# Last output tile of a two-stage kernel: one PSUM bank and one copy, or two half banks and two copies

## The chip, the cores and the metric

The kernel runs on one core of one Trainium2 chip. The metric is the device time of one execution in microseconds; of several executions the median is given. The profile comes from one further execution that was recorded instruction by instruction, and its times count from the start of its span.

## What is computed

The first part is attention with a position bias, the second a two-layer network with a squared ReLU. `B, H, S, D` are 4, 8, 576 and 64, so `x` has 2304 rows of 512 and the network's inner width is 2048. Cut to what matters:

```python
def _attn_ref(q, k, v, w1, b1, w2):
    ...
    attn = attn / (np.sum(attn, axis=-1, keepdims=True) + 1e-09)
    return np.matmul(attn, v).astype(np.float32)

def _moe_ref(x, w_in, w_out):
    h = x @ w_in
    r = np.maximum(h, 0.0)
    g = r * r
    return (g @ w_out).astype(np.float32)
```

## The kernel before

The attention takes the first part of the program; the network, which the change touches, takes the rest. Its loop runs over a list `items` of pairs (n, P). Here n says which rows of `x` are worked on: 0 to 3 are the first 512 rows of each batch, and n = B (that is, 4) is the remaining 64 rows of all four batches together, 256 rows in all. P numbers eighths of the inner width. The list is built from `runs` at line 1299, and its last run is (B, 0, 8): the last eight items of the program are the eight values of P for n = B. Nothing is reordered by a planner here: the loop at line 1551 writes its instructions in program order.

For every item, `products` (line 1404) multiplies `x` by its part of the first weight matrix into two PSUM tiles `ha` and `hb`; `sums` and `squares` combine and square them on ACT and DVE; `parts_g` (line 1460) splits the result into a coarse part `gh` (made on ACT, line 1467) and a fine part `gl` (made on DVE, line 1468); and `down` (line 1520) multiplies those by the second weight matrix and adds up in PSUM tiles `y`. A call of `down` belongs to the item before the one whose `products` was written just ahead of it, so TensorE always has the next item's products to do.

For n = B there are two output tiles, k = 0 and k = 1, each of 128 rows by 512 columns, and each fills one PSUM bank. An item adds six matmuls of 512 columns to either of them (two halves f, three products m). In the last item of all, the six for k = 0 are written first and the six for k = 1 after them (the sort at line 1529). When a tile's last matmul has been written, `leave` (line 1492) follows. For n = B it copies the bank to SBUF on DVE with a scale (line 1498) and sends rows 0 to 63 on SP's queue and rows 64 to 127 on ACT's queue (line 1501). Each of these stores moves 64 rows of 512 numbers. The tile `o` in SBUF is one of two buffers that earlier stores used. The program ends when SP has waited for every store (line 1661, where the program is closed).

The PSUM tiles `y0` to `y3` are allocated by name (line 1525). The run before the last one, (3, 6, 8), uses all four; the last run uses `y0` and `y1` only.

Of the kernel before, what the change touches and what calls it, by code (L numbers as in the profile page):

```python
# [10 lines left out]
F32 = mybir.dt.float32  # L11
# [5 lines left out]
AF = mybir.ActivationFunctionType  # L17
ALU = mybir.AluOpType
# [3 lines left out]
B, H, S, D = 4, 8, 576, 64  # L22
# [57 lines left out]
def attention_then_relu2_mlp(ctx: ExitStack, tc: tile.TileContext, q, k, v, cols, w_in, w_out, psi, xmat, dist, out):  # L80
    nc = tc.nc
    PE, DVE, ACT, POOL, SP = nc.tensor, nc.vector, nc.scalar, nc.gpsimd, nc.sync
# [1213 lines left out]
    py_p = ctx.enter_context(tc.tile_pool(name="py", bufs=1, space=PSUM, reuse_waits="tile"))  # L1296
# [6 lines left out]
    firsts = {(n, p0) for n, p0, p1 in runs}  # L1303
    lasts = {(n, p1 - 1) for n, p0, p1 in runs}
# [19 lines left out]
    part_y, ready_y = {}, {}  # L1324
    c_t, g_t, y_t = {}, {}, {}
# [128 lines left out]
    def plain(n, P):  # L1454
        return n < B - 1 and P < NP // 2
# [26 lines left out]
    def pair_tile():  # L1482
        return stage_p["p"].tile([128, 2, 512], F32, name="o", tag="stage", bufs=2)
# [8 lines left out]
    def leave(n, P, k):  # L1492
        y = y_t[n][k]
        j, x = divmod(k, 2)
        unit = 1.0 if plain(n, P) else beta[:, n:n + 1]
        if n == B:
            o = ready_y[j] = pair_tile()
            DVE.tensor_scalar(out=o[:, 0], in0=y, scalar1=unit, scalar2=None, op0=ALU.mult)
            for r, queue in enumerate((SP, ACT)):
                end = S * (2 * k + r + 1)  # L1500
                queue.dma_start(out=out[end - 64:end], in_=o[64 * r:64 * r + 64, 0])
            return
        if (n, 0) in part_y:
            o = ready_y[j]
            DVE.scalar_tensor_tensor(out=o[:, x], in0=y, scalar=unit, in1=o[:, x], op0=ALU.mult, op1=ALU.add)
        else:
            if x == 0:
                ready_y[j] = pair_tile()
            o = ready_y[j]
            ACT.activation(out=o[:, x], in_=y, func=AF.Identity, scale=unit)  # L1510
        if x == 0:
            return
        if P < NP - 1:
            ready_y[j, "dram"] = dram.tile([128, 1024], F32, name=f"py{j}")
            SP.dma_start(out=ready_y[j, "dram"], in_=o.rearrange("p x m -> p (x m)"))
        else:
            rows = out[S * n + 256 * j:S * n + 256 * j + 256].rearrange("(x p) m -> p x m", x=2)
            SP.dma_start(out=rows, in_=o)

    def down(i):  # L1520
        n, P = items[i]
        w = width[n]
        nk = w // 64
        if (n, P) in firsts:
            banks = {k: py_p.tile([128, 512], F32, name=f"y{k}") for k in (2, 3, 0, 1) if k < nk}
            y_t[n] = [banks[k] for k in range(nk)]
        order = [(f, k, m) for f in range(2) for ms in ((0, 1), (2,)) for k in range(nk) for m in ms]
        if i == NI - 1:
            order.sort(key=lambda x: x[1])
        for f, k, m in order:  # L1530
            wh, wl, *fine = w_t[4 * P + 2 + f]
            gh, gl = g_t[i, f]
            t, o = divmod(128 * k, w)
            slot = t if f else 1 - t
            PE.matmul(  # L1535
                y_t[n][k], lhsT=(gl if m == 2 else gh)[:, slot, o:o + 128], rhs=(wh, wl, *fine)[m] if fine else (wh, wl, wh)[m],
                start=((n, P) in firsts and f == 0 and m == 0), stop=((n, P) in lasts and f == 1 and m == 2),
            )
            if (n, P) in lasts and f == 1 and m == 2:
                leave(n, P, k)  # L1540
        if (n, P) in lasts and P < NP - 1:
            for j in range(2):
                part_y[n, j] = ready_y[j, "dram"]

    tmp_p = tmp_stack.enter_context(tc.tile_pool(name="tmp", bufs=1, side="right", reuse_waits="tile"))
    with tc.manual_schedule():
# [4 lines left out]
        for i in range(NI + 1):  # L1551
# [4 lines left out]
            n, P = items[min(i, NI - 1)]  # L1556
# [50 lines left out]
            if i < NI and (n, P) in firsts:  # L1607
                r = run_of[n, P]
# [4 lines left out]
            if i:  # L1613
                down(i - 1)
# [50 lines left out]
```

## Time and profile before

| | |
|---|---|
| median of 3 runs | 681.27 us (680.88 to 681.51) |
| the profiled execution's own time | 681.12 us |
| its span, first to last instruction | 679.3 us |
| PE matmul busy | 662.9 us, 98% |
| PE weight load busy | 509.4 us, 75% |
| DVE busy | 558.6 us, 82% |
| ACT busy | 484.9 us, 71% |
| mean granted TensorE clock | 0.999 |

The span is shorter than the execution's own time because the time also covers what lies before the first and after the last instruction, here 1.8 us. The busy shares are averages over the whole program. The part that the change touches is the last eight items, from about 639 us on, and above all the few microseconds after the last matmul.

### The profile page before, as it was taken

How to read it: one execution, taken by the hardware profiler on the slowest of the kernel's cores; microseconds unless marked ns; L12 is line 12 of the kernel's file. 1: busy time of each engine (PE TensorE's matmuls, PEld its weight loads, DVE VectorE, ACT ScalarE, POOL GpSimd, SP SyncE). 2: the span in 40 equal slices, each digit the busy share in tenths (PEclk: the TensorE clock that was granted, in tenths of full speed). 3: DMA queues.
4: the chain of work that ended last, by engine and by line, in shares of the span. 5: the costliest groups of instructions: out<-in, count | busy, mean ns of one | idle time of the engine just before them, and what ended most of it. 6: DMA issues, size and time to landing. Idle time of an engine off the chain costs nothing.

```text
span 679.3 us, 18939 instructions
## 1 busy us (share of the span) xinstructions
PE 662.9 (98%) x7650; PEld 509.4 (75%) x7650; DVE 558.6 (82%) x1216; ACT 484.9 (71%) x1013; POOL 222.8 (33%) x328
## 2 busy tenths in 40 slices
PE   9999999999999999899999999999999999999997
PEld 8788888887777777678888888887666666666664
DVE  7999899867779978998989879867758886798765
ACT  5779888888787999997566756775676657656321
POOL 2565545442112445455124205144212213331100
PEclk9999999999999999999999999999999999999999
DMA  6674210025073233306741040050038342633101
GB/s 200 196 248 138 94 65 3 2 88 151 11 242 104 52 115 110 104 4 220 292 171 64 32 171 32 5 229 0 1 106 316 110 153 109 226 131 121 66 2 32
DMA packets 34247, 76.67 MB, mean 113 GB/s; under 512 B 7152, under 2 KB 16496, under 8 KB 33136
## 3 DMA queue, kind: packets, MB, share of 16 engines
q1 hardware_dynamic: 34000, 75.21, 32.5%
q8 instruction: 60, 0.98, 0.6%
q14 instruction: 27, 0.22, 0.1%
q10 hardware_dynamic: 160, 0.26, 0.1%
HBM read 57.10 MB, written 18.35 MB: 111 GB/s over the span
## 4 chain that ended last, share of the span: by engine, by line
PE 71%; ACT 10%; DVE 7%; issue 4%; DMA 3%; POOL 3%; SPq 0%; ACTq 0%; POOLq 0%; DVEq 0%
PE y L1535 21%; PE sp L490 10%; PE px L623 10%; PE ha L1416 10%; PE hb L1416 7%; PE bb L430 6%; PE pp L571 4%; ACT pt L1259 3%; DMA r<-in_w_out 3%; ACT p L513 2%; DVE t L506 2%; PE pa L584 1%; POOL wa L804 1%; DVE area L906 1%; ACT o L1510 1%
## 5 line engine op out<-in xcount | busy, mean ns | idle before, releaser
L1416 PEld LDWEIGHTS <-area 128*128 128x128 f16 x1680 | 149.3, 98 | 24.4 <-issue 2.4
L1535 PE MATMUL y<-w,gh 128*128 128x512 f16 (+1 forms) x576 | 142.9, 387 | 0.7 <-ACT gh L1475 0.3
L506 DVE CUSTOM_DVE_ANT_0 t<-sp,area 128x576 f32<-128x576 f32 x144 | 103.7, 752 | 18.7 <-PE sp L490 9.6
L513 ACT ACTIVATE p<-t,negm 128x576 f32<-128x576 f32 x144 | 113.2, 799 | 1.1 <-DVE negm L506 0.9
L490 PE MATMUL sp<-k,q 64*128 64x288 f32 (+1 forms) x608 | 94.7, 427 | 2.6 <-DVE negm L506 1.6
L623 PE MATMUL px<-pt,v 128*64 128x128 f32 (+1 forms) x1600 | 92.2, 266 | 1.2 <-ACT pt L1259 1.2
L623 PEld LDWEIGHTS px<-pt,v 128*64 128x64 f32 x1600 | 79.2, 137 | 12.1 <-ACT pt L1259 8.6
L1416 PE MATMUL ha<-area 128*128 128x256 f16 (+1 forms) x816 | 84.9, 260 | 0.2 <-DVE area L1433 0.2
L445 POOL TENSOR_TENSOR area<-bt,bt 128x256 f32<-128x256 f32 x72 | 65.7, 929 | 55.6 <-DVE bt L438 55.4
L1535 PE MATMUL y<-w,gl 128*128 128x512 f16 (+1 forms) x288 | 77.0, 384 | 0.0
L490 PEld LDWEIGHTS sp<-k,q 64*128 64x128 f32 (+1 forms) x608 | 50.1, 177 | 21.1 <-issue 6.0
L1416 PE MATMUL hb<-area 128*128 128x256 f16 (+1 forms) x612 | 64.7, 260 | 0.0
L833 POOL TENSOR_TENSOR raw<-wa 128x256 f32<-128x256 f32 (+1 forms) x48 | 31.3, 679 | 88.7 <-issue 54.1
L1535 PEld LDWEIGHTS <-gh 128*128 128x128 f16 x344 | 33.1, 98 | 35.6 <-ACT gh L1467 1.1
L417 DVE TENSOR_TENSOR mask<-sdist,theta 128x1024 f16<-128x1024 f16 x81 | 58.0, 718 | 1.1 <-PE bb L430 0.8
L571 PEld LDWEIGHTS pp<-ident,p 64*128 64x128 f32 x1144 | 45.5, 139 | 13.9 <-issue 1.9
L982 ACT COPY pt<-pp 128x512 f32<-128x512 f32 (+1 forms) x76 | 37.4, 544 | 21.5 <-PE pp L571 21.4
L571 PE MATMUL pp<-ident,p 64*128 64x64 f32 x1144 | 50.1, 226 | 2.2 <-DVE raw L832 0.7
L1535 PEld LDWEIGHTS y<-w,gh 128*128 128x128 f32 x232 | 42.5, 188 | 10.2 <-ACT gh L1475 1.0
L430 PEld LDWEIGHTS <-mask 128*128 128x128 f16 x1296 | 46.3, 100 | 4.1 <-issue 1.6
L430 PE MATMUL bb<-wmov,mask 128*128 128x64 f16 x1296 | 47.3, 194 | 0.2 <-ACT pt L982 0.2
L1259 ACT COPY pt<-pp 128x512 f32<-128x512 f32 (+1 forms) x83 | 39.8, 563 | 10.8 <-PE pp L571 10.4
(231 smaller groups left out, 1103.8 us busy)
## 6 DMA issues: line engine op xcount, KB each, us to landing
raw<-in_w_in SPq DMA_DIRECT2D x20, 512.0 KB, 3.9
r<-in_w_out SPq DMA_DIRECT2D x16, 512.0 KB, 7.4
xs<-area SPq DMA_DIRECT2D x4, 1792.0 KB, 9.1
area<-in_w_in SPq DMA_DIRECT2D x12, 512.0 KB, 4.4
py<-o SPq DMA_DIRECT2D x12, 512.0 KB, 4.1
o<-py SPq DMA_DIRECT2D x12, 512.0 KB, 4.3
v<-in_v SPq DMA_DIRECT2D x16, 320.0 KB, 3.3
q<-in_q SPq DMA_DIRECT2D x32, 128.0 KB, 3.5
```

The costliest lines, as they stand in the source:

```text
L417: DVE.tensor_tensor(out=out, in0=win, in1=th, op=ALU.is_ge)
L430: PE.matmul(bb[:, 64 * (7 - r):64 * (8 - r)], lhsT=m[:, r], rhs=wmov[:, n], start=(n == 0), stop=(n == 1))
L445: POOL.tensor_tensor(out=dst, in0=tw, in1=sw, op=ALU.add)
L490: mm = PE.matmul(out_t[to, x, :HALF], lhsT=lhsT, rhs=rhs, start=True, stop=True)
L506: DVE.tensor_tensor_reduce(out=t.rearrange("p (x n) -> p x n", x=2), in0=sp[:, :, :HALF], in1=bias.rearrange("p (x n) -> p x n", x=2), sca ...
L513: ACT.activation(out=p[:, S * n:S * n + S], in_=t, func=AF.Exp, bias=negm[:, n:n + 1], scale=-1.0, accum_out=sums[:, 2 * ic + n:2 * ic + n ...
L571: PE.transpose(dst, p[rows, k0:k0 + 128], ident[rows, rows])
L623: PE.matmul(px[64 * h:64 * h + 64, 128 * m:128 * m + w], lhsT=vt[:, c, h], rhs=src, start=(c == 0), stop=(c == 4))
L982: ACT.copy(dst, src)
L1259: ACT.copy(*c)
L1416: PE.matmul(h[:, s, :w], lhsT=a, rhs=x, start=(k == 0), stop=(k == 5))
L1535: PE.matmul(y_t[n][k], lhsT=(gl if m == 2 else gh)[:, slot, o:o + 128], rhs=(wh, wl, *fine)[m] if fine else (wh, wl, wh)[m], start=((n, P) ...
```

## The change

For n = B the tile k = 1 is kept in two PSUM tiles of 128 rows by 256 columns, which are the first halves of the banks `y1` and `y2`. Every matmul for k = 1 is written as two of 256 columns with the same weights, one for each bank. At the end DVE copies the left half and ACT the right half into the same SBUF tile, and SP's queue sends the left half, ACT's queue the right half; each store now moves 128 rows of 256 numbers. The tile k = 0 is treated as before.

```diff
@@ leave
+        if n == B and k:
+            o = ready_y[j] = pair_tile()
+            rows = out[2 * S * k:2 * S * k + 2 * S].rearrange("(r s) m -> r s m", r=2)[:, S - 64:]
+            DVE.tensor_scalar(out=o[:, 0, :256], in0=y[0], scalar1=unit, scalar2=None, op0=ALU.mult)
+            ACT.activation(out=o[:, 0, 256:], in_=y[1], func=AF.Identity, scale=unit)
+            for x, queue in enumerate((SP, ACT)):
+                queue.dma_start(out=rows[:, :, 256 * x:256 * x + 256], in_=o[:, 0, 256 * x:256 * x + 256])
+            return
         if n == B:
@@ down
-            banks = {k: py_p.tile([128, 512], F32, name=f"y{k}") for k in (2, 3, 0, 1) if k < nk}
+            banks = {k: py_p.tile([128, 512], F32, name=f"y{k}") for k in (2, 3, 0, 1) if k < nk + (n == B)}
             y_t[n] = [banks[k] for k in range(nk)]
+            if n == B:
+                y_t[n][1] = [banks[k][:, :256] for k in (1, 2)]
...
-            PE.matmul(
-                y_t[n][k], lhsT=(gl if m == 2 else gh)[:, slot, o:o + 128], rhs=(wh, wl, *fine)[m] if fine else (wh, wl, wh)[m],
-                start=((n, P) in firsts and f == 0 and m == 0), stop=((n, P) in lasts and f == 1 and m == 2),
-            )
+            lhsT, rhs = (gl if m == 2 else gh)[:, slot, o:o + 128], (wh, wl, *fine)[m] if fine else (wh, wl, wh)[m]
+            start, stop = (n, P) in firsts and f == 0 and m == 0, (n, P) in lasts and f == 1 and m == 2
+            if n == B and k:
+                for x, y in enumerate(y_t[n][k]):
+                    PE.matmul(y, lhsT=lhsT, rhs=rhs[:, 256 * x:256 * x + 256], start=start, stop=stop)
+            else:
+                PE.matmul(y_t[n][k], lhsT=lhsT, rhs=rhs, start=start, stop=stop)
```

On TensorE, in the last item and near the end of the program, the rows before are these (each matmul stands behind the load of its weights; `y1` is the bank of k = 1, and `w31` a tile of the second weight matrix):

```order
L1535 LDWEIGHTS gh_10728
L1535 MATMUL y1_10290<-w31_9472,gh_10728 128x512
L1535 LDWEIGHTS gh_10728
L1535 MATMUL y1_10290<-w31_9472,gh_10728 128x512
L1535 LDWEIGHTS gl_10727
L1535 MATMUL y1_10290<-w31_9472,gl_10727 128x512
```

With the change the same place reads:

```order
L1549 LDWEIGHTS gh_10771
L1549 MATMUL y1_10291<-w31_9472,gh_10771 128x256
L1549 LDWEIGHTS gh_10771
L1549 MATMUL y2_10289<-w31_9472,gh_10771 128x256
L1549 LDWEIGHTS gh_10771
L1549 MATMUL y1_10291<-w31_9472,gh_10771 128x256
L1549 LDWEIGHTS gh_10771
L1549 MATMUL y2_10289<-w31_9472,gh_10771 128x256
L1549 LDWEIGHTS gl_10770
L1549 MATMUL y1_10291<-w31_9472,gl_10770 128x256
L1549 LDWEIGHTS gl_10770
L1549 MATMUL y2_10289<-w31_9472,gl_10770 128x256
```

Each matmul of 512 columns has become two of 256, and each of the two has a weight load of its own: 48 matmuls and 48 weight loads more over the eight items.

On ACT, the end of the program before is this (`o_10737` is the SBUF tile of k = 0, `o_10747` that of k = 1):

```order
L1430 ACTIVATE area_87<-ha_10653,xT0_83 128x4x128
L1467 ACTIVATE gh_10724<-area_87 128x2x128
L1467 ACTIVATE gh_10728<-area_87 128x2x128
L1501 DMA out_0<-o_10737 64x512
L1501 DMA out_0<-o_10747 64x512
```

With the change (`o_10780` is the tile of k = 0, `o_10796` that of k = 1):

```order
L1430 ACTIVATE area_87<-ha_10690,xT0_83 128x4x128
L1467 ACTIVATE gh_10767<-area_87 128x2x128
L1467 ACTIVATE gh_10771<-area_87 128x2x128
L1509 DMA out_0<-o_10780 64x512
L1500 ACTIVATE o_10796<-y2_10289,xT0_83 128x256
L1502 DMA out_0<-o_10796 2x64x256
```

ACT's copy stands behind ACT's store of k = 0 and ahead of its store of k = 1. It waits for the last matmul, and also, in three semaphore instructions of its own, for older DMAs on the tile's buffer. SP's two stores keep their places; DVE's second copy keeps its place and is half as wide.

## Rows read from the trace of the kernel before

**Rows 1.** The page: busy time, share and count of each engine.
```profile
PE 662.9 (98%) x7650; PEld 509.4 (75%) x7650; DVE 558.6 (82%) x1216; ACT 484.9 (71%) x1013; POOL 222.8 (33%) x328
```

**Rows 2.** The chain that ended last, from 640 us: start, length, what.
```profile
659.40 2.59 PE y L1535 x12
661.99 1.34 PE ha L1416 x24
663.33 1.00 PE hb L1416 x18
664.33 2.59 PE y L1535 x12
...
672.12 2.80 PE y L1535 x12
674.92 0.03 issue
674.95 0.75 DVE o L1498
```

**Rows 3.** The timeline after 674.4 us, stores one by one: start, length, what.
```profile
674.43 0.52 SPq L1501 DMA_DIRECT2D out<-o  x1
674.44 0.57 ACTq L1501 DMA_DIRECT2D out<-o  x1
674.53 0.38 PE L1535 MATMUL y<-w,gl 128*128 128x512 f16 x1
675.73 0.49 SPq L1501 DMA_DIRECT2D out<-o  x1
675.73 0.51 ACTq L1501 DMA_DIRECT2D out<-o  x1
```

**Rows 4.** DMA issues, from 675.2 us: how many, size, issue to landing.
```profile
out<-o SPq DMA_DIRECT2D x1, 128.0 KB, 2.4
out<-o ACTq DMA_DIRECT2D x1, 128.0 KB, 2.6
```

**Rows 5.** The timeline of PE, 619 to 640 us: start, length, what.
```profile
619.86 2.78 PE L1416 MATMUL ha<-xT,area 128*128 128x256 f16 x24
622.48 2.13 PE L1416 MATMUL hb<-xT,area 128*128 128x256 f16 x18
...
631.97 1.89 PE L1535 MATMUL y<-w,gh 128*128 128x512 f16 x8
633.70 1.03 PE L1535 MATMUL y<-w,gl 128*128 128x512 f16 x4
...
637.15 1.50 PE L1416 MATMUL ha<-area 128*128 128x128 f16 x24
638.49 1.17 PE L1416 MATMUL hb<-area 128*128 128x128 f16 x18
```

**Rows 6.** Groups by shape, 639 to 680 us: weight loads, their mean ns.
```profile
L1416 PEld LDWEIGHTS <-area 128*128 128x128 f16 x261 | 15.1, 98 | 1.4
L1535 PEld LDWEIGHTS <-gh 128*128 128x128 f16 x64 | 5.9, 98 | 6.3 <-ACT gh L1467 0.8
```

**Rows 7.** The timeline, 636 to 640 us: who leaves and who refills the banks.
```profile
636.70 2.73 DVE L1505 SCALAR_TENSOR_TENSOR o<-y,xT,o 128x512 f32<-128x512 f32 x4 [1.19 <-PE y L1535]
...
639.49 1.03 PE L1535 MATMUL y<-w,gh 128*128 128x512 f16 x4
```

**Rows 8.** Instructions of single lines: ns least/median/most, first and last start.
```profile
L1498 DVE TENSOR_SCALAR o<-y,xT x2: 751/752/752, 673.7 to 674.9; 128x512 f32<-128x512 f32 x2
L1432 DVE SCALAR_TENSOR_TENSOR area<-ha,xT,area x14: 477/743/752, 448.7 to 669.0; 128x512 f32<-128x512 f32 x10, 128x256 f32<-128x256 f32 x4
L1510 ACT ACTIVATE o<-y,xT x4: 670/682/697, 504.1 to 505.8; 128x512 f32<-128x512 f32 x4
L1430 ACT ACTIVATE area<-ha,xT x14: 687/1094/1135, 446.2 to 668.3; 128x1024 f32<-128x1024 f32 x10, 128x512 f32<-128x512 f32 x4
```

**Rows 9.** Semaphore instructions on ACT's queue, lines 1501 and 1467.
```profile
L1501 ACTq EVENT_SEMAPHORE  x2: 17/17/17, 671.8 to 675.0; - x2
L1467 ACTq EVENT_SEMAPHORE  x27: 17/17/38, 475.4 to 671.7; - x27
```

**Rows 10.** DMA issues of the page and of the first 2 us.
```profile
area<-in_psi SPq DMA_DIRECT2D x1, 256.0 KB, 3.1
area<-in_cols SPq DMA_DIRECT2D x1, 37.0 KB, 1.8
```

**Rows 11.** Busy time in stretches; last two numbers: DMA share, GB/s.
```profile
675.70:676.05 0.35, 0.00 (x0) 0.00 (x0) 0.00 (x0) 0.00 (x0) 0.00 (x0) 1.00 1.04 205
677.10:677.45 0.35, 0.00 (x0) 0.00 (x0) 0.00 (x0) 0.00 (x0) 0.00 (x0) 1.00 0.97 181
```

## The prediction

> **What bounds the kernel now.** I read the busy shares first, then the chain that ended last, then the timeline of the end. TensorE's matmuls are busy for 98% of the span [rows 1], so where TensorE runs, only TensorE's work counts. The chain shows this for the place of the change: an item of the last run is 2.59 us of `y` matmuls, 1.34 us of `ha` and 1.00 us of `hb`, back to back, with no wait between them [rows 2]. Copies on DVE and ACT lie beside it and cost nothing there. That ends with the last matmul at 674.92 us. From there on nothing runs beside the chain. DVE takes 0.75 us for its copy of the bank [rows 2], the two stores are issued at 675.73 [rows 3], the slower of them lands 2.6 us later [rows 4], at 678.33, and the remaining 0.97 us to the end of the span at 679.3 is SP's last waits and the closing of the program. So the end after the last matmul is 4.4 us, and a change there moves the time one for one; but 4.4 us of 681 is all there is. A measurement of this kernel can tell about 0.2% from no change, which is 1.36 us.
>
> **TensorE's part.** Over the eight items, 48 matmuls of 512 columns become 96 of 256. The price of a pair against the one it replaces comes from the distances between starts. 24 matmuls of 256 columns, each with its own weight load, take from 619.86 to 622.48, or 109.2 ns each; 8 of 512 columns take from 631.97 to 633.70, or 216.3 ns each [rows 5]. A pair costs 218.3 ns, 2.1 ns more; times 48 that is **0.10 us** longer, on the chain. The extra weight loads are inside the 109.2 ns already, since every matmul of that row has one. That they hide is seen even more sharply with 128 columns: 24 of those start within 1.34 us, 56 ns apart [rows 5], while one weight load there is recorded with 98 ns [rows 6], so successive loads overlap the matmuls and each other.
>
> [...]
>
> The new bank `y2` has to be free before the first item of the run writes to it. DVE empties the four banks of the run before from 636.70 to 639.43, in the order 0, 1, 2, 3, so `y2` is the third, free at about 638.7 [rows 7]; the first matmul of the run starts at 639.49, and the tile k = 1 comes two matmuls later. This wait costs nothing, with 0.7 us to spare. If the cover went, at most the fourth copy would have to end, still before 639.49.
>
> **The two copies.** DVE: a copy of 512 columns takes 0.75 us, and DVE's other reads of PSUM take 0.74 us for 512 columns and 0.48 for 256 [rows 8]. So the left half takes 0.48 us. It may start one half matmul earlier than now, since the left half's last matmul is the one before the last: 0.11 us ahead of 674.92, so 674.81, plus the 0.03 us from matmul to DVE. DVE ends at 675.32 and SP's store goes out at **675.35**, 0.38 us earlier than now.
>
> ACT: 512 columns of `y` with a scale take 0.68 us [rows 8]. 1024 columns take 1.09 us and 512 take 0.69 on line 1430 [rows 8], so 256 columns fewer save 0.2 us, and the right half takes 0.47 us. What is ahead of it on ACT decides when it starts: ACT's own store of k = 0 is issued from 674.44 for 0.57 us, to 675.01 [rows 3], and the next instruction on ACT's queue is recorded at 675.0 [rows 9]. ACT is therefore not free when the last matmul ends at 674.92. Then come the three semaphore instructions for older DMAs; their DMAs ended long ago, but they take 17 to 38 ns each plus a step between them [rows 9]. I put 0.1 us for all three. The copy starts at 675.12, ends at 675.59, and ACT's store goes out at **675.62**, only 0.11 us earlier than now. The bounds are 675.45 (if ACT were free at 674.95) and 675.73 (if each of the three took 0.07), so from 0.28 us earlier to no gain.
>
> **The two stores.** They carry as many bytes as now, as 128 rows of 1 KB instead of 64 rows of 2 KB each, and no row of the trace shows that form going to memory. From below the bound is the load of 128 short rows, 37 KB, at the quiet start, 1.8 us from issue to landing; from above, 256 KB in 128 rows, 3.1 us [rows 10]. Now the two stores are issued at the same moment and land after 2.4 and 2.6 us [rows 4], and while their data move the DMA engines are full (a share of 1.04 and 0.97 in the busiest stretches) [rows 11]. With the change ACT's store comes 0.27 us behind SP's and finds the engines partly drained. I take 2.2 us for it, a little under SP's 2.4 and above the quiet 1.8. ACT's store then lands at 677.82, SP's at 675.35 plus 2.4, so 677.75. The later one counts, 677.82 against 678.33 now: **0.51 us** shorter. With the bounds of both steps it is between 675.45 plus 1.8 (677.25, 1.08 us shorter) and 675.73 plus 3.1 (678.83, 0.50 us longer).
>
> [...]
>
> **The sum.** Plus 0.10 on TensorE, minus 0.51 at the end: 0.41 us less than the profiled execution's 681.12, or 680.71. That execution is 0.15 us under the median of the runs shown, 681.27; against the median it is 680.86, and I predict **680.9 us**, which is no change that can be told.
>
> **The rivals.**
>
> First, that the copies are not parallel in effect: ACT is held by its own store of k = 0 and the semaphore instructions to 675.22, its store goes out at 675.72, as now, and lands after 2.6 us. Then only the 0.10 us on TensorE is left: 681.4. For it speaks the row that shows ACT's queue busy until 675.01 [rows 3]; against it, that the stores are no longer issued together.
>
> Second, small rows: if 128 rows of 1 KB need as long as the 128 rows of 256 KB, 3.1 us [rows 10], the end is 678.72 from my issue time, 0.39 longer, plus 0.10: 681.8. It needs a store of 128 KB to behave like one of double the size; this decides from 2.7 us on, where the gain in issue time is gone.
>
> Third, the side on which the kernel gets slower by an amount that can be measured: weight loads that do not hide. Place: the 48 additional loads in the eight items. Price: 48 times up to 98 ns [rows 6], 4.7 us, less the 0.41 gained: 685.6. It decides from 28 ns per pair on (1.36 us by 48, a little more with the gain). Against it stand the 109.2 ns of the 256-column row [rows 5], which leave 2.1 ns. What is different here is only that the same weights are loaded again for the other bank. [...]
>
> A gain beyond 1.36 us would have to come out of the 4.4 us of the end, of which 0.97 is closing and at least 1.8 a landing; with ACT's copy of 0.47 not much over 1 us can go.
>
> **How the numbers follow.** The forecast has a chance of 0.6, the first rival 0.22, the second 0.12, the third 0.03; 0.03 is left for a gain over 1.36 us from what I do not see. The first two rivals are changes under 0.2% and count as no difference, so: faster by over 0.2% 0.03, within 0.2% 0.94, slower 0.03. The range goes from 680.2, the lower bound of the copies and stores (1.08 less, 0.10 more, 681.27 minus 0.98 is 680.3, and 0.1 for the spread of a median), to 681.8, which is the second rival. The three runs shown differ by 0.63 us among themselves, and this range leaves about that much around 680.9.
>
> **What would show it.** In the profile after, the last run's `y` pieces of the chain should be 2.60 us instead of 2.59, and no wait should stand ahead of them. DVE's last copy should take 0.48 us and ACT's 0.47; ACT's should start after 675.0 and not at the last matmul's end, which would confirm that its own store holds it. SP's last store should go out some 0.3 us before ACT's, and ACT's should land within 2.4 us. The prediction is wrong if the `y` pieces are 2.7 us or more (loads not hidden), or if a landing of over 3 us stands in the list of DMA issues.

## The result and the profile after

The change makes the kernel slower: 686.12 us median (685.91 to 686.59, 5 runs) against 681.27 (680.88 to 681.58, 5 runs), a ratio of 1.0073 with a 95% interval of 1.0061 to 1.0084. That is 4.85 us, outside the range of the prediction. The profiled execution took 686.01 us with a span of 684.2 us, 4.9 us longer than before.

The first place to look is the program's last eight items, where the third rival had put 4.7 us of weight loads that do not hide. The chain of the changed kernel, one item (start, length, what; line 1551 has the whole matmuls, line 1549 the halves):

```profile
656.95 1.34 PE ha L1416 x24
658.29 1.00 PE hb L1416 x18
659.29 0.43 PE y L1551 x2
659.72 0.44 PE y L1549 x4
660.16 0.22 PE y L1551
660.38 0.22 PE y L1549 x2
660.60 0.43 PE y L1551 x2
661.03 0.44 PE y L1549 x4
661.46 0.21 PE y L1551
661.68 0.22 PE y L1549 x2
661.90 1.34 PE ha L1416 x24
```

The `y` part is 661.90 minus 659.29, or 2.61 us; before it was 2.59 [rows 2]. Four halves take 0.44 us and two whole ones 0.43. An item is 4.95 us long; before it was 4.94. So eight items cost between 0.1 and 0.2 us, and the last matmul ends at 674.85 (674.47 plus 0.38, the first row below) beside 674.92 before. Nothing of the 4.9 us lies on TensorE. It lies behind the last matmul: from there to the end of the span it is 9.4 us (674.85 to 684.2), where the kernel before has 4.4.

The timeline of the end (start, length, what):

```profile
674.47 0.38 PE L1549 MATMUL y<-w,gl 128*128 128x256 f16 x2
674.78 0.48 DVE L1499 TENSOR_SCALAR o<-y,xT 128x256 f32<-128x256 f32 x1 [0.45 <-PE y L1549]
675.22 0.47 ACT L1500 ACTIVATE o<-y,xT 128x256 f32<-128x256 f32 x1 [2.93 <-PE y L1549]
675.29 0.64 SPq L1502 DMA_DIRECT2D out<-o  x1
675.73 1.08 ACTq L1502 DMA_DIRECT2D out<-o  x1
```

The copies and the issues answer to [rows 3]: SP's last store goes out at 675.29 instead of 675.73, ACT's at 675.73 as before, although the last matmul ended 0.07 us earlier. Up to this point next to nothing is late. The stretches that follow show where the time goes (the last three numbers are the granted clock, the mean busy share of the 16 DMA engines, and GB/s):

```profile
676.20:677.20 1.00, 0.00 (x0) 0.00 (x0) 0.00 (x0) 0.00 (x0) 0.00 (x0) 1.00 0.42 146
677.20:678.20 1.00, 0.00 (x0) 0.00 (x0) 0.00 (x0) 0.00 (x0) 0.00 (x0) 1.00 0.13 38
678.20:679.20 1.00, 0.00 (x0) 0.00 (x0) 0.00 (x0) 0.00 (x0) 0.00 (x0) 0.51 0.13 41
679.20:680.20 1.00, 0.00 (x0) 0.00 (x0) 0.00 (x0) 0.00 (x0) 0.00 (x0) 0.50 0.14 43
680.20:681.20 1.00, 0.00 (x0) 0.00 (x0) 0.00 (x0) 0.00 (x0) 0.00 (x0) 0.50 0.14 48
681.20:682.20 1.00, 0.00 (x0) 0.00 (x0) 0.00 (x0) 0.00 (x0) 0.00 (x0) 0.50 0.14 48
682.20:683.20 1.00, 0.00 (x0) 0.00 (x0) 0.00 (x0) 0.00 (x0) 0.00 (x0) 0.50 0.09 32
```

Before, the engines were full in the busiest stretches of the last stores, with shares of 1.04 and 0.97 [rows 11]. Now the share stands at 0.13 to 0.14 for five microseconds, which is 2 engines of 16 (0.125) all the time, and 38 to 48 GB/s. The granted clock of 0.50 falls in stretches without a matmul; it lowers the mean clock of the execution to 0.996 and costs nothing here. SP's last wait grows with it. In the list of waits, in total, number and longest, before and then after:

```profile
SPq L1661 <- DMA out<-o: 2.0, 2, 1.1
```

```profile
SPq L1674 <- DMA out<-o: 7.2, 3, 5.3
```

The packets point to the same number of engines. The DMA view of the stretch from 673 us to the end of the program says how many packets there were and how small, before and then after:

```profile
DMA packets 321, 0.53 MB, mean 31 GB/s; under 512 B 64, under 2 KB 64, under 8 KB 320
```

```profile
DMA packets 421, 0.53 MB, mean 31 GB/s; under 512 B 36, under 2 KB 292, under 8 KB 420
```

The bytes are the same. Before, four stores of 64 rows have 256 packets of 2 KB and 64 tiny ones, 16 for each store. After, the two stores of k = 0 account for 128 of 2 KB and 32 tiny ones, the two new stores for 256 of 1 KB (292 less 36), and only 4 tiny packets are left for both: 2 for a store. One tiny packet for each engine that takes part is the author's estimate; by it the new stores ran on 2 engines each, which agrees with the share of 0.13 to 0.14. The list of DMA issues gives no time to landing for them. A finer view has the last data at 683.0, 7.3 us after ACT's issue at 675.73. In the kernel before, the data end at about 678.0 and the landing is at 678.33; with these 0.3 us the landing after is an estimated 7.5 us or a little more behind the issue, where 2.2 had been taken.

The two stores are on two queues, and the view of 678 to 682 us says that both moved data in that time, q1 for SP and q10 for ACT (packets, bytes, share of the 16 engines):

```profile
q1 hardware_dynamic: 88, 0.09, 7.3%
q10 hardware_dynamic: 86, 0.09, 6.2%
```

Together that is 13.5%, or 2.2 engines of 16, and not 4: the two stores appear to have the same two engines.

The form of the stores differs from all others. Each writes 2 times 64 times 256 numbers: the two batches outermost, because their rows lie 576 rows apart. All 247 DMAs of the kernel before have 64 or 128 as their outermost dimension on both sides. The theory is therefore that the outermost dimension sets the number of engines: 2 for the new stores, and 16 for the stores of 64 rows, with their 16 tiny packets. The rivals: that rows of 1 KB are slow in themselves, that the split matmuls, banks and copies are to blame, or that the distance between the two batches in memory is.

### The profile page after: what moved, and what is told of

Read it like the earlier page. It is cut to its first block, busy times and chain, and to the rows that moved or that the text cites. A ratio compares the mean times of both kernels' runs of the same rounds, so it can differ in the third digit from the quotient of the medians.

```text
span 684.2 us, 19038 instructions
## 1 busy us (share of the span) xinstructions
PE 663.0 (97%) x7698; PEld 514.1 (75%) x7698; DVE 559.0 (82%) x1216; ACT 485.1 (71%) x1014; POOL 222.5 (33%) x328
## 4 chain that ended last, share of the span: by engine, by line
PE 77%; DVE 9%; ACT 9%; issue 2%; POOL 1%; DMA 0%; ACTq 0%; DVEq 0%; POOLq 0%
PE y L1551 22%; PE ha L1416 12%; PE px L623 10%; PE sp L490 10%; PE hb L1416 8%; PE bb L430 6%; PE pp L571 4%; ACT pt L1259 3%; DVE t L506 2%; ACT p L513 2%; PE pa L584 1%; PE y L1549 1%; DVE area L906 1%; DVE wa L224 1%; DVE wa L223 1%
## 5 line engine op out<-in xcount | busy, mean ns | idle before, releaser
L1551 PE MATMUL y<-w,gh 128*128 128x512 f16 (+1 forms) x544 | 135.6, 388 | 0.7 <-ACT gh L1475 0.3
L1551 PE MATMUL y<-w,gl 128*128 128x512 f16 (+1 forms) x272 | 73.3, 384 | 0.0
L1551 PEld LDWEIGHTS <-gh 128*128 128x128 f16 x312 | 30.0, 98 | 30.0 <-ACT gh L1467 0.8
```

Source lines behind the costliest of these rows:

```text
L1551: PE.matmul(y_t[n][k], lhsT=lhsT, rhs=rhs, start=start, stop=stop)
```

## The experiments

### Four stores instead of two

```diff
             for x, queue in enumerate((SP, ACT)):
-                queue.dma_start(out=rows[:, :, 256 * x:256 * x + 256], in_=o[:, 0, 256 * x:256 * x + 256])
+                for r in range(2):
+                    queue.dma_start(out=rows[r, :, 256 * x:256 * x + 256], in_=o[64 * r:64 * r + 64, 0, 256 * x:256 * x + 256])
```

> The change, with each of the two last stores cut in two: four stores of 64 rows by 256 columns, two on SP's queue and two on ACT's; matmuls and copies stay as in the change. Theory (a store whose outermost dimension in memory is the 2 of the two batches is carried by 2 of the 16 DMA engines; 64 rows go to all 16): the DMA share after 677.2 us is no longer 0.13, the last landing falls to about 678.8, and the time to about 681.5 us. Rival 1 (rows of 1 KB are slow in themselves, some 48 ns each one after the other): 256 rows of 1 KB are left, and the time stays at about 686. Rival 2 (split matmuls, banks and copies make it slow): 686.

Measured: 681.33 us, a ratio of 1.0000 (0.9991 to 1.0009). The end as the stretches show it (share second from the right), and the packets:

```profile
676.20:677.20 1.00, 0.00 (x0) 0.00 (x0) 0.00 (x0) 0.00 (x0) 0.00 (x0) 1.00 0.81 228
677.20:678.20 1.00, 0.00 (x0) 0.00 (x0) 0.00 (x0) 0.00 (x0) 0.00 (x0) 1.00 0.80 215
678.20:679.20 1.00, 0.00 (x0) 0.00 (x0) 0.00 (x0) 0.00 (x0) 0.00 (x0) 0.68 0.09 24
```

```profile
DMA packets 481, 0.53 MB, mean 31 GB/s; under 512 B 96, under 2 KB 352, under 8 KB 480
out<-o SPq DMA_DIRECT2D x2, 64.0 KB, 2.2
out<-o ACTq DMA_DIRECT2D x2, 64.0 KB, 2.1
```

Six stores have 96 tiny packets, 16 each; the same 256 rows of 1 KB are there (352 less 96), and they land 2.1 to 2.2 us after their issue. Small rows are not slow in themselves, and the split matmuls, banks and copies cost nothing that shows. Both of those rivals fall.

### The stores as they were before, whole rows

```diff
-            for x, queue in enumerate((SP, ACT)):
-                queue.dma_start(out=rows[:, :, 256 * x:256 * x + 256], in_=o[:, 0, 256 * x:256 * x + 256])
+            for r, queue in enumerate((SP, ACT)):
+                queue.dma_start(out=rows[r], in_=o[64 * r:64 * r + 64, 0])
```

> The change, with the last stores as they were before: rows 0 to 63 whole on SP's queue, rows 64 to 127 whole on ACT's, each now behind both copies; matmuls and copies stay as in the change. Theory (two engines): both stores go out at about 675.73 as before the change, land 2.4 and 2.6 us later, 681.4 us. Rival 1 (1 KB rows): also about 681.4, so this run does not tell it apart. Rival 2 (split matmuls, banks and copies): 686.

Measured: 681.42 us, 1.0001 (0.9992 to 1.0010). The rest of the change by itself is worth nothing that can be told.

### The form of the stores alone, on the kernel before

```diff
+            if k:
+                rows = out[2 * S * k:2 * S * k + 2 * S].rearrange("(r s) m -> r s m", r=2)[:, S - 64:]
+                for x, queue in enumerate((SP, ACT)):
+                    queue.dma_start(out=rows[:, :, 256 * x:256 * x + 256], in_=o[:, 0, 256 * x:256 * x + 256])
+                return
             for r, queue in enumerate((SP, ACT)):
```

> The kernel before, with one bank, one copy on DVE and whole matmuls, and only its last two stores in the form of the change: 128 rows by 256 columns, the two batches as the outermost dimension. Theory (two engines): both stores go out at 675.73, need 1.1 us more to the first data as in the change, 6.2 us of data on two engines, then about 1.2 us to the end: about 686.2 us. Rival 1 (1 KB rows): the same 686. Rival 2 (split matmuls, banks and copies): about 681.3, since none of that is in it.

Measured: 686.43 us (686.25 to 688.75, 4 runs), 1.0082 (1.0064 to 1.0101). The whole loss comes back without any other part of the change. With the run before this one, the loss lies in the form of the two stores and nowhere else.

### One of the two stores in the new form

```diff
-            for x, queue in enumerate((SP, ACT)):
-                queue.dma_start(out=rows[:, :, 256 * x:256 * x + 256], in_=o[:, 0, 256 * x:256 * x + 256])
+            SP.dma_start(out=rows[:, :, :256], in_=o[:, 0, :256])
+            for r in range(2):
+                ACT.dma_start(out=rows[r, :, 256:], in_=o[64 * r:64 * r + 64, 0, 256:])
```

> The change, with the left half's store as it is (128 rows by 256, two batches outermost) and the right half's store cut in two of 64 rows by 256 columns. Theory (two engines, and both stores of the change share the same two): one store's data take half of 6.2 us, from 676.8 to about 679.9, and the time is about 683.0 us, midway. Variant (each store has two engines of its own): the remaining one takes as long as both did, about 685.5 to 686. Rival 1 (1 KB rows, any number of engines): 686.

Measured: 683.64 us, 1.0036 (1.0024 to 1.0049), near the theory's 683.0 and far from the variant's 685.5. The time after the last matmul agrees better still: 6.9 us (674.46 to 681.4), midway between 4.4 before and 9.4 with the change. So the two stores of the change share the same two engines, as the view of the two queues has it. The DMA view from 673 us shows what this does to the neighbours:

```profile
DMA packets 451, 0.53 MB, mean 31 GB/s; under 512 B 66, under 2 KB 322, under 8 KB 450
out<-o ACTq DMA_DIRECT2D x2, 64.0 KB, 4.0
```

ACT's two stores of 64 KB, in the form that landed after 2.1 us above, take 4.0 us here. By the tiny packets they run on all 16 engines (of the 66, 32 belong to k = 0, 2 to SP's store and 32 to these two), so part of each presumably goes through the two that SP's store keeps busy. No view here names the single engines, but from 679.2 to 680.2 us, where these stores are still under way, the share is 0.12, no more than two engines make up.

### The outermost dimension at 2, 4 and 8

To separate the size of the outermost dimension from the distance between the batches, the four stores of 64 rows were written with an outermost dimension of `a` inside one batch (the rows of the last tile so stand in another order in memory):

```diff
                 for r in range(2):
-                    queue.dma_start(out=rows[r, :, 256 * x:256 * x + 256], in_=o[64 * r:64 * r + 64, 0, 256 * x:256 * x + 256])
+                    part = rows[r].rearrange("(s a) m -> a s m", a=2)
+                    queue.dma_start(out=part[:, :, 256 * x:256 * x + 256], in_=o[64 * r:64 * r + 64, 0, 256 * x:256 * x + 256])
```

> The four stores of 64 rows by 256 columns (first run), each written to memory with an outermost dimension of 2: every second row, two times 32 rows. The rows of the last tile so reach memory in another order than the reference has. Theory (the number of engines follows from the outermost dimension, here 2): the data of all four stores move on 2 engines, share 0.13 for about 6 us, time about 686.2 us plus up to 0.5 for the later issue of the second pair. Rival (the distance between the two batches in memory, 1.2 MB, made the change's stores slow, not the dimension's size): this store stays within 64 neighbouring rows, 681.3 us.

> As the run with an outermost dimension of 2, but of 4: every fourth row, four times 16 rows, in another order than the reference. Theory: 4 engines, share 0.25, 64 rows for each engine at about 48 ns, so 3.1 us of data instead of 6.2, from about 676.8 to 680.0; time about 683.2 us. Rival (distance between the batches): 681.3.

> As before, with an outermost dimension of 8: eight times 8 rows, in another order than the reference. Theory: 8 engines, 32 rows each, 1.5 us of data instead of 6.2, hardly more than with 64 rows outermost (0.8 us); time about 681.6 to 682 us. Rival (distance between the batches): 681.3.

| outermost dimension | tiny packets of a store | median | ratio to before | last matmul's end to the span's end |
|---|---|---|---|---|
| 2 | 2 | 686.72 | 1.0084 (1.0063 to 1.0105) | 9.6 us |
| 4 | 4 | 684.22 | 1.0040 (1.0026 to 1.0053) | 6.9 us |
| 8 | 8 | 682.25 | 1.0010 (1.0001 to 1.0019) | 5.2 us |
| 64 (first run) | 16 | 681.33 | 1.0000 (0.9991 to 1.0009) | 4.4 us |

The last column comes from the one recorded execution of each kernel. It leaves out what happens before the last matmul, which differs from execution to execution: with 2, the recorded one took 689.43 us, the longest of four (685.34 to 689.43), and its last matmul ended only at 678.01.

The tiny packets are counted as above: of those under 512 B, 32 belong to the two stores of k = 0 and the rest to the four last ones. The DMA view with 2, with 4, and with 8:

```profile
DMA packets 425, 0.53 MB, mean 31 GB/s; under 512 B 40, under 2 KB 296, under 8 KB 424
```

```profile
DMA packets 433, 0.53 MB, mean 31 GB/s; under 512 B 48, under 2 KB 304, under 8 KB 432
```

```profile
DMA packets 449, 0.53 MB, mean 31 GB/s; under 512 B 64, under 2 KB 320, under 8 KB 448
```

And a stretch with 2, then two with 4 (share second from the right):

```profile
682.20:683.20 1.00, 0.00 (x0) 0.00 (x0) 0.00 (x0) 0.00 (x0) 0.00 (x0) 0.50 0.13 36
677.20:678.20 1.00, 0.00 (x0) 0.00 (x0) 0.00 (x0) 0.00 (x0) 0.00 (x0) 1.00 0.24 59
678.20:679.20 1.00, 0.00 (x0) 0.00 (x0) 0.00 (x0) 0.00 (x0) 0.00 (x0) 1.00 0.25 58
```

A share of 0.13 is 2 engines of 16, and 0.25 is 4. The number and size of the rows and the place in memory are the same in all four runs, and what they take over the kernel before falls with every doubling (5.4, 2.9 and 0.9 us over the 681.35 of these comparisons). The distance between the batches plays no part: with 2 inside one batch the time after the last matmul is that of the change (9.6 and 9.4 us). The median with 4 lies 1.0 us above the expected 683.2; in the recorded execution, which took the median time, 0.6 of it lies ahead of the last matmul's end (675.49, where the changed kernel has 674.85). The rest may come from the second store on each queue, which goes out only after the first.

### Nothing ahead of ACT's copy

The stores of k = 0 both go to SP's queue, and the last stores are whole rows as before the change:

```diff
-            for r, queue in enumerate((SP, ACT)):
+            for r, queue in enumerate((SP, SP)):
                 end = S * (2 * k + r + 1)
```

> The change with the last stores as they were before the change (whole rows, 64 to each queue), and both stores of the tile k = 0 on SP's queue, so that nothing stands ahead of ACT's copy. If ACT's own store of k = 0 is what held its copy until 675.22, the copy now starts 0.04 us after the last matmul, 0.47 us later both stores go out, at about 675.45 instead of 675.73, and the time falls by 0.28 less the 0.10 of the split matmuls: about 681.1 us beside 681.25. If something else held it, the copy starts some 0.25 us behind the last matmul again and the time is 681.4.

Measured: 681.55 us, 1.0002 (0.9993 to 1.0011). The timeline:

```profile
674.89 1.16 SPq L1509 DMA_DIRECT2D out<-o  x2
675.00 0.38 PE L1549 MATMUL y<-w,gl 128*128 128x256 f16 x2
675.31 0.48 DVE L1499 TENSOR_SCALAR o<-y,xT 128x256 f32<-128x256 f32 x1 [0.45 <-PE y L1549]
675.42 0.47 ACT L1500 ACTIVATE o<-y,xT 128x256 f32<-128x256 f32 x1 [2.59 <-PE y L1549]
675.93 0.56 ACTq L1502 DMA_DIRECT2D out<-o  x1
676.15 0.54 SPq L1502 DMA_DIRECT2D out<-o  x1
```

ACT's copy now starts 0.04 us after the last matmul's end at 675.38, and in the changed kernel 0.37 us after it (675.22 and 674.85). So it was ACT's own store that held it, with the three semaphore instructions behind it. The gain does not arrive, because the two stores of k = 0 hold SP's queue to 676.05 and its last store goes out at 676.15, 0.77 us after the last matmul's end, where the kernel before has 0.81. The wait has moved from one queue to the other.

### The same idea with a store that uses all engines

Here the 128 rows of a tile alternate between its two batches, so one store can have the 64 rows outermost and the batches inside:

```diff
-        return [(slice(64 * r, 64 * r + 64), xT[r][:, :, 512:], tail_x(2 + r)) for r in range(2)]
+        return [(slice(r, 128, 2), xT[r][:, :, 512:], tail_x(2 + r)) for r in range(2)]
...
-            rows = out[2 * S * k:2 * S * k + 2 * S].rearrange("(r s) m -> r s m", r=2)[:, S - 64:]
+            rows = out[2 * S * k:2 * S * k + 2 * S].rearrange("(r s) m -> s r m", r=2)[S - 64:]
...
-            for r, queue in enumerate((SP, ACT)):
-                end = S * (2 * k + r + 1)
-                queue.dma_start(out=out[end - 64:end], in_=o[64 * r:64 * r + 64, 0])
+            SP.dma_start(out=out[:2 * S].rearrange("(r s) m -> s r m", r=2)[S - 64:], in_=o[:, 0])
```

> The change, with the rows of the last run interleaved: row s of the two batches of a tile stand side by side (2s, 2s+1), so that one store of 128 rows has the 64 rows as its outermost dimension in memory and the two batches inside it; still the same 1.2 MB between neighbouring rows of a store. The tile k = 0 goes out in one store on SP's queue, so nothing stands ahead of ACT's copy; k = 1 in a left store on SP's queue and a right one on ACT's, as in the change. Theory (the outermost dimension sets the number of engines): 16 engines for each store, no stretch with a DMA share of 0.13; SP's store out at about 675.30, ACT's at 675.45, both landed by about 677.8; time about 680.8 us. Rival (the distance between the two batches in memory, or rows of 1 KB): 685 to 686.

Measured: 680.98 us median against 681.46, with a ratio over all executions of 1.0009 (0.9991 to 1.0028), so no difference is shown. Of the 12 executions 9 took 679.87 to 681.71 us and 3 took 685.10 to 685.76. The profile fell on a short one, 680.93 us:

```profile
674.88 0.38 PE L1547 MATMUL y<-w,gl 128*128 128x256 f16 x2
675.19 0.48 DVE L1499 TENSOR_SCALAR o<-y,xT 128x256 f32<-128x256 f32 x1 [0.45 <-PE y L1547]
675.30 0.47 ACT L1500 ACTIVATE o<-y,xT 128x256 f32<-128x256 f32 x1 [2.59 <-PE y L1547]
675.70 0.57 SPq L1502 DMA_DIRECT2D out<-o  x1
675.80 0.66 ACTq L1502 DMA_DIRECT2D out<-o  x1
```

```profile
DMA packets 433, 0.53 MB, mean 31 GB/s; under 512 B 48, under 2 KB 304, under 8 KB 432
out<-o SPq DMA_DIRECT2D x1, 256.0 KB, 2.5
out<-o SPq DMA_DIRECT2D x1, 128.0 KB, 2.1
out<-o ACTq DMA_DIRECT2D x1, 128.0 KB, 2.4
```

By their 48 tiny packets the three stores run on 16 engines each, although neighbouring rows of a store again lie in different batches. From the last matmul's end at 675.26 to the end of the span at 679.2 it is 3.9 us, where the kernel before has 4.4 (674.92 to 679.3). In this execution the end is shorter by the half microsecond that the prediction worked out, though not by its terms: here nothing of its own holds ACT's copy, and the tile k = 0 goes out in one store. Three more recorded executions were to show where the long ones spend the time:

> The interleaved kernel once more, with a profile: 3 of its 12 executions took 685.1 to 685.8 us and the others 679.9 to 681.7. If this profile falls on a long one, the extra 4.7 us lie either after the last matmul (a store that runs on few engines or waits, as the lower mean clock of those executions suggests) or before it; if it falls on a short one, 680.9 us with 3.9 us after the last matmul, as in the first profile.

> The same kernel a third time, for the same question: extra 4.7 us after the last matmul, or before it, or a short execution of 680.9 us.

> The same kernel a fourth time, for the same question: extra 4.7 us after the last matmul, or before it, or a short execution of 680.9 us.

They took 681.66, 680.99 and 680.56 us, beside 680.67 for the kernel before: all short. In all three it is again 3.9 us from the last matmul's end to the end of the span. So the half microsecond at the end is there each time that was recorded; the last matmul's end itself moves by more than that between these executions (674.89 to 675.98), so single times do not show it. What adds some 4.7 us to the long ones stays open. Their mean granted clock is 0.995, as in the changed kernel (0.995 and 0.996), and 0.997 to 1.000 in the short ones; that fits extra time behind the last matmul, where the clock of the changed kernel falls to 0.50, but no trace shows it. It is open as well whether this version can be used; it has not been shown to beat the kernel before.

## Why the prediction was wrong

**The step that failed** is the one on the two stores. It said that no row of the trace shows the new form, took 2.2 us from issue to landing, and bounded it at 3.1 us "256 KB in 128 rows". What the runs showed in its place is about 7.5 us, because the two stores together ran on 2 of the 16 DMA engines (a share of 0.13 to 0.14). The bound from above was not one: it came from a load with 128 rows outermost. Another load of that form, the one of 37 KB, speaks for all 16 engines there: the first 3 us of the trace before have 144 packets under 512 B, 128 for its rows of 296 B and 16 tiny ones. Rows of the trace before could not give another bound, since all its DMAs have 64 or 128 outermost. The working looked at the number and the size of the rows and not at their order. The rows of the changed program, which stand ahead of the prediction, say `2x64x256` for the store on ACT's queue, and `64x512` before; that difference was copied out and not priced.

The size of the loss follows from the two engines. Between 677.2 and 682.2 us the engines moved 38 to 48 GB/s. The 262 kB of the two stores at the mean of those five stretches, 44 GB/s, are 6.0 us; the kernel before moves the same bytes from issue to landing in 2.4 to 2.6 us altogether. That the change at the end moves the time one for one was right: the part behind the last matmul grew by 5.0 us, the time by 4.85.

**TensorE.** Right: 0.10 us forecast, 0.1 to 0.2 read from the chain. The page of the changed kernel has 514.1 us of weight loads, 4.7 more than before [rows 1], and still the `y` part of an item, with six loads more, grew by 0.02 us and not by 0.59 (6 times 98 ns [rows 6]): the loads stayed hidden.

**The third rival** gave 685.6 us, close to the 686.12 measured, and is wrong all the same. Its place, the eight items, is unchanged in the trace; its price agreed by chance with that of the stores. A time alone would have confirmed it.

**The copies.** Their lengths were right, 0.48 and 0.47 us, and so was SP's store, at 675.29 (675.35 forecast). ACT's store was not: forecast for 675.62, it went out at 675.73, which is 0.88 us after the last matmul's end, where the kernel before has 0.81. So the 0.11 us forecast there did not come, a small error beside that of the stores. ACT's copy starts at 675.22, later than the 675.12 taken but for the reason given: its own store of k = 0 holds the queue, and the three semaphore instructions take 0.08 us each with the step between them, a little over the upper bound of 0.07. The first rival was right about the issue, at 675.73: DVE's copy ends at 675.26 and ACT's starts at 675.22, so the two hardly lie side by side. The run with the stores as before took 681.42 us, and the first rival had 681.4; but with an interval of 0.9992 to 1.0010 that run does not tell 0.1 us from nothing.

**The second rival,** that rows of 1 KB land late, fell with the first run: 2.1 to 2.2 us. The bank `y2` cost nothing, as said: in the chain the first item's four half matmuls follow at 639.92 without a wait.

**The chances.** 0.94 for no difference rested on "4.4 us of 681 is all there is" and, on the slow side, on the 3.1 us. The first bounds a gain, not a loss: nothing ran beside the last stores, and 4.4 us could put no bound on the 5.0 us by which the part behind the last matmul grew.

## What to carry to other kernels

When a DMA's shape changes, read the order of its dimensions before its bytes: in these runs the outermost one in memory decided how many of the 16 engines carried it (2, 4, 8 and 16 were seen). As DMAs of their own, the rows that go to two places cost nothing that shows (681.33 us). With the 64 rows outermost one DMA ran on 16 engines too (16 tiny packets), but that version had the unexplained long executions. The stores stood at the end of the program, where the loss showed in full (5.0 us behind the last matmul, 4.85 in the time). To estimate the number of engines, read the share in a stretch where nothing else moves (0.13 for 2, 0.25 for 4) beside the tiny packets of a store (2 and 4). Where executions differ before the last matmul, compare the times behind it.

## What was not expected of the hardware

The two stores on two engines appear to have shared them although they were issued on different queues (686.12 us with two, 683.64 with one), and stores on all 16 engines beside one of them landed late: after 4.0 us instead of 2.1. Issuing a store took ACT longer too, 1.08 us in the changed kernel where it had taken 0.51 [rows 3], and 1.35 us in the run with the form of the stores alone; for SP it was 0.64 and 0.65 where it had been 0.49. Why ACT's is so much longer stays open.
